# Sixteen words each of k and v, read on ScalarE's queue behind the two transfers of mu

## The chip, the cores and the metric

The kernel runs on one core of one Trainium2 chip. The metric is the device time of one execution in microseconds, as the median of the runs; one further execution is recorded by the hardware profiler, and its trace is what the prediction reads.

## What is computed

Linear attention for 8 batches of 8 heads (576 positions, 64 features per head), followed by an RWKV channel mix over the joined heads (512 features, 1024 hidden). All inputs and the output are float32. Cut to what matters:

```python
q_s = softmax(q, axis=-1)                 # over the features
k_s = softmax(k, axis=2)                  # over the positions
kv  = einsum('bhsd,bhse->bhde', k_s, v)
x   = einsum('bhsd,bhde->bhse', q_s, kv)  # then the heads side by side: [8, 576, 512]

x_prev = x shifted by one position, zeros first
xk = mu_k * x + (1 - mu_k) * x_prev
xr = mu_r * x + (1 - mu_r) * x_prev
k  = maximum(xk @ w_k, 0)
v  = k * k @ w_v
out = sigmoid(xr @ w_r) * v
```

## The kernel before

**Order.** The kernel lists some 700 steps, each with an engine, a planned cost and what it must follow. A fixed order, written out as `ORDER`, gives the steps their places; a planner (`Plan.run`) works out when each would start, and `Plan.emit` issues the instructions in order of those planned starts. Each engine runs its own instructions strictly in that order. The planned costs and latencies (`cost`, `lat`) therefore matter only where they change the order of the starts. In the gaps that the plan sees on TensorE before the first step of the channel mix, `emit` puts fill matmuls (`warm`, L320): products of the identity that nobody reads, whose number is fixed when the kernel is built.

**Tiles.** The work goes by batch `b` and half `u` (four heads). A tile of q, k or v is 128 partitions of two runs of 9 x 64 floats (576 KB), loaded by `load` (L327) on SyncE's queue; each partition's run is 2304 bytes, so that one half of a tile is a contiguous block of 128 x 2304 bytes. For batches 0 and 1 the steps are:

- ScalarE: `exp` (L332) of q and of k, out of `ldq` and `ldk` into `eq` and `ek`.
- VectorE: the sums of q (L342), their inverse, and the scaled q (`qs`, L347).
- TensorE: the transposes of `qs` (`turn_q`, L361), which ScalarE or VectorE then copy to `qT`.
- GpSimd: the cast of v to bf16 (`cast_v`, L238), out of `ldv` into `vb`, in two halves.
- TensorE: `kv` (L378), the product of `ek` and `vb`; VectorE scales it by mu into `kvm` (`weigh_kv`, L391 and L393).
- TensorE: `x_mixed` (L410), the product of `qT` and `kvm`, which gives the mixed rows at once; ScalarE or VectorE copy them to `xk` and `xr`.
- TensorE: `up` (L454) with w_k, then `gate` (L473) with w_r and `down` (L490) with w_v.

**The start.** SyncE's queue issues, in this order: q (0,0), q (0,1), k (0,0), v (0,0), k (0,1), the two halves of v (0,1), the two halves of w_k (L296), w_r (L301), and then the tiles of batch 1. ScalarE's queue begins with `load_mu` (L252): the two vectors mu_k and mu_r, each as four rows of 128 floats into the tile `mus`. The table load for exp, and then exp of q (0,0), are next on ScalarE. `mask_mu` (L263, VectorE) and `spread_mu` (L269 and L271, TensorE) make of `mus` the forms that `weigh_kv` reads; `keep_mu` (L277, L278) copies them out on ScalarE.

**Semaphores.** The build gives the transfers of both queues eight completion semaphores in turn. An instruction that issues a transfer waits until the transfer eight places before it has landed.

**The step that the change touches** is planned as

```python
a = pl.step("ACT", 0.9, load_mu, lat=4.0)
```

and `scrap`, the new tile, stands in the constants' pool between `mus` and `half`; `wk_bf`, `wr_bf` and `wv_bf` (the bf16 weights) are allocated behind them.

Of the kernel before, what the change touches and what calls it, by code (L numbers as in the profile page):

```python
# [9 lines left out]
ACT = mybir.ActivationFunctionType  # L10
# [3 lines left out]
F32 = mybir.dt.float32  # L14
# [128 lines left out]
def kernel(  # L143
# [12 lines left out]
    nc = tc.nc  # L156

    B, H, S, D = q.shape
# [3 lines left out]
    J = S // 64  # L162
# [11 lines left out]
    const = ctx.enter_context(tc.tile_pool(name="const", bufs=1))  # L174
# [19 lines left out]
    ident = const.tile([128, 128], BF16, name="ident")  # L194
    identf = const.tile([128, 128], F32, name="identf")
    mus = const.tile([8, 128], F32, name="mus")
    half = const.tile([8, 2, 64], F32, name="half")
    mine = const.tile([8, 4], F32, name="mine")
    halves = const.tile([8, 2], F32, name="halves")
# [13 lines left out]
    pl = Plan({k: len(t) for k, t in bufs.items()})  # L213
# [4 lines left out]
    def sl(kind, *key):  # L218
        if (kind, *key) not in slot:
            slot[(kind, *key)] = pl.slot(kind)  # L220
        return slot[(kind, *key)]
# [28 lines left out]
    def load_mu():  # L250
        for i, src in enumerate((moe_mu_k, moe_mu_r)):
            nc.scalar.dma_start(out=mus[4 * i:4 * i + 4, :],  # L252
                                in_=bass.AP(tensor=src.tensor, offset=src.offset,
                                            ap=[[128, 4], [1, 128]]))

    def pick():
        rows = identf[0:8, 0:8].rearrange("p (a h) -> p a h", h=2)
        nc.vector.reduce_sum(out=halves[:], in_=rows.rearrange("p a h -> p h a"), axis=AX.X)  # L258
        nc.vector.tensor_copy(out=half[:], in_=halves[:, :, None].to_broadcast((8, 2, 64)))
        nc.vector.reduce_sum(out=mine[:], in_=rows, axis=AX.X)  # L260
# [282 lines left out]


    ev["prep"] = pl.step("POOL", 1.5, prepare)
    a = pl.step("ACT", 0.9, load_mu, lat=4.0)
    p = pl.step("DVE", 0.5, pick, after=[ev["prep"]])
    p = pl.step("DVE", 0.7, mask_mu, after=[a, p], uses=[sl("th", "musb")])
    ev["mup"] = p = pl.step("PE", 2.2, spread_mu, after=[p],
# [153 lines left out]
    a = pl.step("DVE", 1.2, watch, after=[e for k, e in ev.items() if k[0] == "mix"])  # L703
    a = pl.step("PE", 0.2, gather, after=[a], uses=[sl("two", "flag")], lat=0.3)
    a = pl.step("DVE", 0.2, judge, after=[a], uses=[sl("two", "flag")])
    a = pl.step("PE", 0.1, read_flag, after=[a], lat=6.0)
# [122 lines left out]
```

## Time and profile before

| | |
|---|---|
| median of three runs | 201.28 us (201.13, 201.28, 202.19) |
| profiled execution | 200.41 us |
| its span, first to last instruction | 198.5 us |
| mean granted TensorE clock | 0.985 |
| TensorE busy | 187.5 us (94%) |
| VectorE, ScalarE, GpSimd busy | 148.1, 139.6, 31.3 us |
| moved by the DMA engines | 46.88 MB, mean 236 GB/s |

In a timeline row the columns are: start in us from the span's start, duration in us, engine, line, operation, what it writes and reads, how many instructions are merged in the row, and in brackets the idle time of the engine before it with what ended it. `SPq` and `ACTq` are the queues of SyncE and ScalarE; their rows are the issues of transfers, not the transfers. In a row of windows the columns are the stretch, its length, the busy time of PE, PEld, DVE, ACT and POOL with counts, the granted clock, the busy share of the 16 DMA engines and the GB/s that they moved. A row of a DMA queue gives packets, MB and the time of its packets as a share of 16 engines over the stretch.

### The profile page before, as it was taken

To read this page: it belongs to the slowest core of one execution; us is meant where nothing else is said; L and a number is where in the kernel's file an instruction comes from. 1 tells how busy PE (TensorE), PEld (TensorE's weight loads), DVE (VectorE), ACT (ScalarE), POOL (GpSimd) and SP (SyncE) were. 2 spreads that over 40 slices of the span, in tenths; PEclk is the share of its full clock that TensorE was granted. 3 is DMA by queue.
4 is the path that set the end of the run, shared out by engine and by line. 5 is a ranking of instruction groups with operands and counts; after the bars stand their busy time and mean duration, and the time that the engine had idled before them with its cause. 6 is when DMAs were issued, how large, how long until landed. Compare 5 with 4: busy or idle time off the path is not lost. (4 is left out here: it accounts for less than half of the span.)

```text
span 198.5 us, 4750 instructions
## 1 busy us (share of the span) xinstructions
PE 187.5 (94%) x1908; PEld 113.8 (57%) x1932; DVE 148.1 (75%) x230; ACT 139.6 (70%) x206; POOL 31.3 (16%) x43
## 2 busy tenths in 40 slices
PE   6699999999999999999999999999999999999990
PEld 4466865756546754654666546755574657564450
DVE  1978699999898999966999799799696474524230
ACT  3574699778999969968879687997857667452200
POOL 2073514622002300400016002300200000000000
PEclk9889999999999999999999999999999999999997
DMA  5999999989999499978999899984948022151555
GB/s 206 359 397 387 391 390 390 388 300 204 260 345 278 106 275 345 267 163 218 386 396 262 191 342 275 290 198 101 310 116 192 14 55 54 42 118 33 117 129 154
DMA packets 35897, 46.88 MB, mean 236 GB/s; under 512 B 16280, under 2 KB 16544, under 8 KB 35872
## 3 DMA queue, kind: packets, MB, share of 16 engines
q1 hardware_dynamic: 35456, 46.02, 78.2%
q10 hardware_dynamic: 416, 0.53, 1.0%
q8 instruction: 16, 0.26, 0.6%
q14 instruction: 9, 0.07, 0.1%
HBM read 33.56 MB, written 9.44 MB: 217 GB/s over the span
## 5 line engine op out<-in xcount | busy, mean ns | idle before, releaser
L454 PE MATMUL two<-xk,wk_bf 128*128 128x288 bf16 x512 | 68.0, 286 | 0.0
L490 PE MATMUL one<-wv_bf,k 128*128 128x512 bf16 (+1 forms) x283 | 65.1, 373 | 1.1 <-PEq L793 0.4
L454 PEld LDWEIGHTS <-wk_bf 128*128 128x128 bf16 x512 | 49.7, 98 | 17.6
L459 ACT ACTIVATE rel<-two 128x576 bf16<-128x576 f32 x64 | 40.5, 652 | 21.3 <-PE two L454 21.1
L490 PEld LDWEIGHTS <-k 128*128 128x128 bf16 x296 | 28.6, 98 | 31.0 <-issue 0.6
L238 POOL CAST vb<-ldv 128x1152 bf16<-128x1152 f32 (+1 forms) x20 | 22.3, 1131 | 101.0 <-DMA ldv<-in_v_dram 101.0
L473 PE MATMUL one<-wr_bf,xr 128*128 128x512 bf16 x133 | 35.7, 379 | 0.8 <-issue 0.3
L440 ACT ACTIVATE aw<-two,om 128x575 bf16<-128x575 f32 x48 | 32.9, 746 | 5.0 <-PE two L432 5.0
L496 DVE SCALAR_TENSOR_TENSOR ot<-th,one 128x512 f32<-128x512 f32 x33 | 22.3, 680 | 14.5 <-PE one L490 14.4
L478 ACT ACTIVATE th<-one 128x512 f32<-128x512 f32 x36 | 21.4, 600 | 12.9 <-PE one L473 12.7
L469 DVE TENSOR_TENSOR k<-rel 128x1152 bf16<-128x1152 bf16 x26 | 21.7, 839 | 5.0 <-ACT rel L459 5.0
L342 DVE TENSOR_REDUCE rs<-eq 128x18 f32<-128x1152 bf16 x16 | 21.5, 1346 | 2.1 <-ACT eq L332 2.1
L445 DVE SCALAR_TENSOR_TENSOR xk<-two,mu,aw 128x576 bf16<-128x576 f32 x24 | 19.3, 812 | 4.5 <-ACT aw L440 3.9
L347 DVE TENSOR_TENSOR qs<-eq,inv 128x1152 bf16<-128x1152 bf16 x16 | 22.3, 1396 | 0.3
L445 DVE SCALAR_TENSOR_TENSOR xr<-two,mu,aw 128x576 bf16<-128x576 f32 x24 | 19.3, 810 | 2.5 <-ACT aw L440 2.5
L332 ACT ACTIVATE eq<-ldq 128x1152 bf16<-128x1152 f32 x16 | 18.5, 1168 | 2.3 <-DMA ldq<-in_q_dram 2.3
L473 PEld LDWEIGHTS <-xr 128*128 128x128 bf16 x144 | 13.2, 98 | 11.6 <-issue 0.2
L332 ACT ACTIVATE ek<-ldk 128x1152 bf16<-128x1152 f32 x16 | 18.8, 1172 | 1.1 <-DMA ldk<-in_k_dram 1.1
L320 PE MATMUL one<-ident 128*128 128x256 bf16 x58 | 10.5, 330 | 1.8 <-DVE halves L258 1.8
L320 PEld LDWEIGHTS <-ident 128*128 128x128 bf16 x58 | 6.3, 120 | 4.1 <-DVE halves L258 1.8
L378 PEld LDWEIGHTS <-ek 64*64 64x64 bf16 x576 | 6.2, 107 | 3.2 <-ACT rel L459 1.3
L378 PE MATMUL two<-vb,ek 64*64 64x65 bf16 x576 | 7.7, 194 | 0.2 <-POOL vb L238 0.2
(54 smaller groups left out, 86.3 us busy)
## 6 DMA issues: line engine op xcount, KB each, us to landing
ldq<-in_q_dram SPq DMA_DIRECT2D x16, 576.0 KB, 6.6
ldk<-in_k_dram SPq DMA_DIRECT2D x16, 576.0 KB, 7.4
out_dram<-ot SPq DMA_DIRECT2D x66, 128.0 KB, 3.3
ldv<-in_v_dram SPq DMA_DIRECT2D x14, 576.0 KB, 9.2
k<-in_moe_w_k_dram SPq DMA_DIRECT2D x2, 1024.0 KB, 11.3
k<-in_moe_w_v_dram SPq DMA_DIRECT2D x2, 1024.0 KB, 13.7
ldv<-in_v_dram SPq DMA_DIRECT2D x4, 288.0 KB, 11.0
xr<-in_moe_w_r_dram SPq DMA_DIRECT2D x1, 1024.0 KB
```

The lines of the kernel that those rows point to most:

```text
L238: return {"DVE": nc.vector, "POOL": nc.gpsimd}[eng].tensor_copy(out=out, in_=in_)
L332: nc.scalar.activation(out=at("e" + n, b, u)[:].rearrange("p j (h d) -> p h j d", h=2), in_=at("ld" + n, b, u)[:].rearrange("p h (j d) -> ...
L342: nc.vector.reduce_sum(out=rs[:], in_=at("eq", b, u)[:].rearrange("p j (h d) -> p (j h) d", h=2), axis=AX.X)
L347: nc.vector.tensor_tensor(out=at("qs", b, u)[:].rearrange("p j (h d) -> p (j h) d", h=2), in0=at("eq", b, u)[:].rearrange("p j (h d) -> p ...
L440: nc.scalar.activation(out=at("aw", b, u, h, w)[:, 1:S], in_=x_of(b, u, h)[:, 1:S], func=ACT.Copy, scale=om[:, c:c + 1])
L445: nc.vector.scalar_tensor_tensor(out=blend(b, w)[:, 2 * u + h, :], in0=x_of(b, u, h)[:, 64:64 + S], scalar=mu[:, c:c + 1], in1=at("aw", b, ...
L454: nc.tensor.matmul(ps[:, a, 0:HS], lhsT=wk_bf[:, ct, 128 * f:128 * f + 128], rhs=xk[:, ct, HS * a:HS * a + HS], start=(ct == 0), stop=(ct ...
L459: nc.scalar.activation(out=at("rel", b, f // 2)[:, f % 2, :].rearrange("p (a c) -> p a c", a=2), in_=at("two", "up", b, f)[:, :, 0:HS], fu ...
L469: nc.vector.tensor_tensor(out=dst, in0=r[:], in1=r[:], op=ALU.mult)
L473: nc.tensor.matmul(at("one", "rp", i, m)[:], lhsT=at("xr", i)[:, ct, 128 * m:128 * m + 128], rhs=wr_bf[:, ct, :], start=(ct == 0), stop=(c ...
L490: nc.tensor.matmul(at("one", "vp", i, m, a)[:, cols], lhsT=at("k2", i)[:, f, 128 * m:128 * m + 128], rhs=wv_bf[:, f, cols], start=(f == 0) ...
L496: nc.vector.scalar_tensor_tensor(out=at(kept(i, m), i, m)[:, cols], in0=at("th", i, m)[:, cols], scalar=1.0, in1=at("one", "vp", i, m, a)[ ...
```

## The change

`load_mu` issues two more transfers behind the two of mu: from k, then from v, sixteen single words. The words stand 8 x 9 x 64 floats apart, which is every eighth partition's run of the first half of tile (0,0). They go to every eighth partition of the new tile `scrap`, k's to its first column and v's to its second. Nothing reads `scrap`. The planned cost of the step rises from 0.9 to 2.0 and its planned latency falls from 4.0 to 2.9, so that its planned end with latency stays at 4.9. The instructions of TensorE, VectorE, GpSimd and SyncE stay the same and in the same order, and ScalarE's gain the two issues. The turn of the eight semaphores moves by two from the load of q (0,1) on, and the tiles allocated behind `scrap` lie 32 bytes higher.

```diff
     mus = const.tile([8, 128], F32, name="mus")
+    scrap = const.tile([128, 2], F32, name="scrap")
     half = const.tile([8, 2, 64], F32, name="half")
...
                                 in_=bass.AP(tensor=src.tensor, offset=src.offset,
                                             ap=[[128, 4], [1, 128]]))
+        for i, src in enumerate((k, v)):
+            nc.scalar.dma_start(out=scrap[0:128:8, i:i + 1],
+                                in_=bass.AP(tensor=src.tensor, offset=src.offset,
+                                            ap=[[8 * J * D, 16], [1, 1]]))
...
-    a = pl.step("ACT", 0.9, load_mu, lat=4.0)
+    a = pl.step("ACT", 2.0, load_mu, lat=2.9)
```

## The prediction

> **What bounds the kernel now.** I read the page first, for which engine is full and when.
>
> ```profile
> span 198.5 us, 4750 instructions
> PE 187.5 (94%) x1908; PEld 113.8 (57%) x1932; DVE 148.1 (75%) x230; ACT 139.6 (70%) x206; POOL 31.3 (16%) x43
> PEclk9889999999999999999999999999999999999997
> DMA  5999999989999499978999899984948022151555
> ```
>
> TensorE is busy 94% of the span and at a high granted clock; the transfers are as full as they get in the first seventy microseconds. The change touches only the first ten, so the question is what sets the start of TensorE's unbroken work. I therefore read TensorE's timeline from 8 to 25 us next.
>
> ```profile
> 8.73 1.14 PE L361 MATMUL two<-ident,qs 128*128 128x128 bf16 x9 [1.50 <-DVE qs L347]
> 9.66 2.92 PE L320 MATMUL one<-ident 128*128 128x256 bf16 x17
> 12.76 0.48 PE L378 MATMUL two<-vb,ek 64*64 64x65 bf16 x36 [0.17 <-POOL vb L238]
> 13.17 0.68 PE L361 MATMUL two<-ident,qs 128*128 128x128 bf16 x9
> ...
> 15.33 0.39 PE L320 MATMUL one<-ident 128*128 128x256 bf16 x2
> 15.65 0.69 PE L410 MATMUL two<-qT,kvm 64*64 64x256 bf16 x20
> ...
> 19.67 5.06 PE L454 MATMUL two<-xk,wk_bf 128*128 128x288 bf16 x40
> 24.57 0.49 PE L320 MATMUL one<-ident 128*128 128x256 bf16 x3
> 24.90 0.38 PE L473 MATMUL one<-wr_bf,xr 128*128 128x512 bf16 x1
> ```
>
> This is the view that decides the case. TensorE works in a fixed order, and between the real steps it runs fill matmuls on the identity (L320), a fixed number of them. From 8.73 us on the queue is packed: the only idle entries are 1.50 us before the first transposes, which waited for q, and 0.17 us before the first k-by-v products (L378), which waited for the cast of v. Everything between is either work or fill that stays where it is when data come sooner. Next, who feeds those two waits: the timeline of the first 16 us, all engines.
>
> ```profile
> 0.84 0.58 ACTq L252 DMA_DIRECT2D mus<-in_moe_mu_k_dram  x1
> 1.46 0.26 ACTq L252 DMA_DIRECT2D mus<-in_moe_mu_r_dram  x1
> 1.76 1.28 ACT L332 ACT_TABLE_LOAD   x1 [1.76 <-issue]
> ...
> 4.43 1.16 ACT L332 ACTIVATE eq<-ldq 128x1152 bf16<-128x1152 f32 x1 [1.39 <-DMA ldq<-in_q_dram]
> 4.71 0.68 DVE L263 TENSOR_TENSOR th<-mus,mine 8x512 f32<-8x512 f32 x1 [2.63 <-DMA mus<-in_moe_mu_r_dram]
> 6.48 1.16 ACT L332 ACTIVATE eq<-ldq 128x1152 bf16<-128x1152 f32 x1 [0.89 <-DMA ldq<-in_q_dram]
> 7.31 1.36 DVE L347 TENSOR_TENSOR qs<-eq,inv 128x1152 bf16<-128x1152 bf16 x1
> 8.70 1.16 ACT L332 ACTIVATE ek<-ldk 128x1152 bf16<-128x1152 f32 x1 [1.05 <-DMA ldk<-in_k_dram]
> 10.23 3.72 POOL L238 CAST vb<-ldv 128x576 bf16<-128x576 f32 x4 [8.57 <-DMA ldv<-in_v_dram]
> ```
>
> The first q tile lands at 4.43, the second at 6.48, the first k tile at 8.70, the first v tile at 10.23: steps of 2.05, 2.22 and 1.53 us for equal sizes. So something in front of k costs up to 0.52 + 0.69 = 1.21 us against v's pace, on whichever of the 16 DMA engines is last. The windows show the same as a mean over all of them.
>
> ```profile
> 2.80:4.80 2.00, 2.00 (x12) 1.44 (x10) 0.09 (x1) 0.61 (x2) 0.00 (x0) 1.00 1.04 400
> 4.80:6.60 1.80, 1.57 (x8) 0.78 (x6) 1.57 (x2) 0.91 (x2) 0.00 (x0) 1.00 0.98 309
> 6.60:10.40 3.80, 2.30 (x18) 1.80 (x18) 3.66 (x7) 2.70 (x4) 0.17 (x1) 0.70 1.02 386
> ```
>
> The last number is GB/s, the one before it the share of the DMA engines that is busy. From 4.8 to 6.6 us, where the first k rows begin, the engines are as busy (0.98) but move 309 GB/s where 400 went before: (400 - 309) / 400 x 1.8 = 0.41 us lost per engine. After that it is 386. A first touch of k that costs time is what this looks like; v shows little of it.
>
> **The change part by part.** *The two reads, on the DMA engines.* They move 32 words and their completions. The window of the first 12 us gives the price of a packet on ScalarE's queue:
>
> ```profile
> q10 hardware_dynamic: 16, 0.00, 0.2%
> ```
>
> Sixteen packets are 0.2% of 16 engines x 12 us = 0.38 us, or 24 ns each. Some 64 more packets are 1.5 us of engine time, 0.1 us for each of the 16: at most 0.1 us later for everything behind. That is the price if a word of k costs no more than a row of mu; the bound above is a word that stalls its engine like k's first rows did, up to 1.21 us; the bound below is that they take k's stall out of the way, 0.41 us in the mean and up to 1.21 us at the last engine. No row shows such a read. I take the mean, 0.41 us sooner for k and v, because nothing but the position in the stream (k's first rows) explains the dip, and the words lie in that tile.
>
> When do they go? mu_r was issued by 1.72 and VectorE still waited for it until 4.71, about when the first q tile had landed (4.43), so a small transfer on ScalarE's queue is served behind the q rows already queued. The read of k then goes between the first and the second q tile, one tile ahead of k.
>
> *What the sooner landing is worth.* k first: its exp moves from 8.70 to about 8.3, but the ACT step behind it evicts the transposes that TensorE ends at 8.73 + 1.14 = 9.87, so ScalarE gains nothing. v: the casts move from 10.23 to about 9.8, and the product at 12.76 loses its wait for POOL. How far can it move? The fill ahead of it ends at 9.66 + 2.92 = 12.58; the L410 step at 15.65 shows that a ready step starts 0.07 before the modelled end of its fill (15.33 + 0.39 = 15.72). So it can start at 12.51: **0.25 us sooner, and no more**, whether v lands 0.41 or 1.21 us sooner. Behind it all is order and fill, so the 0.25 stays to the end.
>
> *The issues on ScalarE.* The two new issues stand ahead of the table load. At mu's 0.26 to 0.58 each they take 0.52 to 1.17 us, and the table load, from 1.76, has 1.39 us of idle time behind it before q lands: hidden, with 0.22 us left at the dear end. If the cover goes, each further 0.1 us reaches exp, the q chain and the transposes at 8.73 in full.
>
> *The waits on SyncE's queue.* The build hands out eight completion semaphores in turn and lets a transfer wait for the eighth before it. Two more transfers shift this by two from the second q load on: the second k load now waits for mu_k, the halves of v for the first q tile and mu_r, and the halves of w_k for the two small reads; from w_r on each waits for what it waited for before. SyncE's timeline of the kernel before:
>
> ```profile
> 2.90 0.59 SPq L327 DMA_DIRECT2D ldk<-in_k_dram  x1
> 3.54 0.97 SPq L327 DMA_DIRECT2D ldv<-in_v_dram  x2
> 4.55 1.64 SPq L296 DMA_DIRECT2D k<-in_moe_w_k_dram  x2
> 6.47 3.51 SPq L301 DMA_DIRECT2D xr<-in_moe_w_r_dram  x1
> ```
>
> The halves of v go out at 4.43 instead of 3.54, and w_k when the words are in, at worst with k and v, around 8.7 to 10.2 instead of 4.55. Queued behind SyncE's wait stand w_r and the next q loads. Their cover is the data already queued: GpSimd's timeline shows w_k's first use at 15.93 and its second half's at 19.18.
>
> ```profile
> 15.93 1.17 POOL L238 CAST wk_bf<-k 128x512 bf16<-128x512 f32 x2 [1.98 <-DMA k<-in_moe_w_k_dram]
> 19.18 0.62 POOL L238 CAST wk_bf<-k 128x512 bf16<-128x512 f32 x1 [2.08 <-DMA k<-in_moe_w_k_dram]
> 21.89 2.55 POOL L238 CAST wr_bf<-xr 128x1024 bf16<-128x1024 f32 x2 [2.10 <-DMA xr<-in_moe_w_r_dram]
> ```
>
> The spacing of these landings, about 3 us per half, says that the first half's rows begin to move near 13 us and the second's near 16, so an issue at 10 leaves 3 us. Taken at nothing. If that cover went, w_r is next: its casts end at 21.89 + 2.55 = 24.44 and TensorE uses them at 24.90, so 0.46 us of lateness is free there.
>
> *The tile.* `scrap` pushes the tiles allocated behind it 32 bytes up, the three weight tiles among them. No row tells whether a matmul minds; I take nothing, and leave it in the tail.
>
> **The sum.** The profiled execution took 200.41 us, its span of 198.5 plus 1.91. Minus 0.25, plus 0 for issues, waits and tile: 200.16. The median of the runs, 201.28, stands 0.87 above that execution, so the forecast is 201.28 - 0.25 = 201.03, said as **201.0 us**. A difference of 0.5% (1.0 us) is about what a measurement here can tell from no change; the three runs lie 1.06 us apart.
>
> **Rivals.** *The stall only moves* (chance 0.25). The words meet the stall instead of k's rows, one tile sooner, and the engine that waits for them carries nothing else meanwhile. Then the second q tile lands later, by 0.41 us (6.48 to 6.9), k and v when they did, plus the 0.1 of the packets. The second q tile can afford it: its exp ends at 7.64 and ScalarE then idles until 8.70. v has no cover, so the 0.1 counts: 201.4 us. For it: the busy share stayed at 0.98 while the rate fell, so a stalled engine counts as busy and does nothing else. Against it: a pending word need not hold a row of another queue. [...]
>
> *Slower: the words pay and save nothing* (0.20). If the dip belongs to the rows read and not to a first touch of the tensor, the words stall in their own right and k's rows again. The place is the first cast of v on POOL at 10.23, which TensorE already waits for; from the first 0.1 us on, lateness there counts in full. The price is a k-like stall at the last engine, 1.21 us: 202.5 us; at the mean, 0.41, it is 201.7. [...] Against it: the steps between later tiles are back at 1.53.
>
> *Slower: the issues outgrow their cover* (0.06). At 0.82 each, w_k's price on SyncE (1.64 for two), the table load ends 0.25 us late: 201.5; it would need 1.2 each to pass 1 us. [...]
>
> *Faster by over 1 us* (0.09). The granted clock is part of it: transposes take 1.14 us at 8.73 and 0.68 at 13.17, so TensorE ran slow around 9 us. If sooner data kept the clock up, those transposes give 0.46 us, the fills more, and v's 1.21 us would then count in full: 200.1. Against it: the idle 1.50 us before 8.73 hangs on q, which the change leaves alone.
>
> **How the numbers follow.** The forecast has 0.40, the rivals 0.25, 0.20, 0.06 and 0.09. The range runs from 200.2, near the fast rival, to 202.5, the slow one's price. Within 0.5% means 200.27 to 202.29: the forecast and the moved stall (0.65) less 0.12 for the scatter of the runs, plus the cheap ends of the slow rivals (0.07) make 0.60. Slower by over 0.5%: 0.19 from the slow rivals and 0.05 from scatter, 0.24. Faster: 0.09 and 0.07, 0.16.
>
> **What would show it.** Right: the rate from 4.8 to 6.6 us is up towards 400, k's exp starts before 8.5 and v's cast before 10.0, L378 starts at about 12.5 with no wait for POOL, and the first L454 at about 19.4. Moved stall: the dip sits before 4.8 us and v's cast is at 10.2 to 10.3. Slow: v's cast after 10.6 and L378 behind it. The issues: the table load ends after 4.43. Wrong altogether: L454 first starts where it did, and the time differs by over 1 us, which the tile's place or the later waits would have to explain.

## The result, and the profile after

The changed kernel takes 202.84 us (median of 15 runs, 201.74 to 204.22), the kernel before, run beside it, 201.61 us (15 runs). The ratio is **1.0085, 95% interval 1.0058 to 1.0112**: slower by about 1.7 us, or by 1.2 us if the two medians are taken (their quotient is 1.0061), where 201.0 us, no measurable change, was forecast. 202.84 lies above the top of the stated range, 202.5. The ratio leaves out executions that lie more than 1.5% above the fastest of the same kernel. The profiled execution took 202.59 us, its span 200.8.

First the same parts of the page, now of the changed kernel.

```profile
span 200.8 us, 4752 instructions
PE 188.6 (94%) x1908; PEld 113.9 (57%) x1932; DVE 148.9 (74%) x230; ACT 139.6 (70%) x206; POOL 33.9 (17%) x43
PEclk9969999999999999999999999999999999999996
DMA  6999999989998399997997999955948031242535
```

TensorE is busy 1.1 us longer than before, of which 0.9 us lie ahead of the channel mix, in time in which it was idle before; GpSimd is busy 2.6 us longer, the rest and the clock (0.983, before 0.985) are about as they were. So the 2.3 us by which the span grew have to be looked for in waits. The prediction looked at the start. TensorE's timeline there, changed kernel (its lines lie 5 further on than before):

```profile
8.82 0.68 PE L366 MATMUL two<-ident,qs 128*128 128x128 bf16 x9 [1.13 <-DVE qs L352]
9.34 3.46 PE L325 MATMUL one<-ident 128*128 128x256 bf16 x17
12.81 0.60 PE L383 MATMUL two<-vb,ek 64*64 64x65 bf16 x36
...
19.78 5.06 PE L459 MATMUL two<-xk,wk_bf 128*128 128x288 bf16 x40
```

The channel mix (L459) starts at 19.78 us instead of 19.67: 0.11 us of the loss, no more. What feeds it, from the timeline of all engines and the windows:

```profile
1.76 0.58 ACTq L257 DMA_DIRECT2D scrap<-in_k_dram  x1
2.38 0.60 ACTq L257 DMA_DIRECT2D scrap<-in_v_dram  x1
3.01 1.28 ACT L337 ACT_TABLE_LOAD   x1 [3.01 <-issue]
4.53 1.16 ACT L337 ACTIVATE eq<-ldq 128x1152 bf16<-128x1152 f32 x1 [0.24 <-DMA ldq<-in_q_dram]
6.33 1.16 ACT L337 ACTIVATE eq<-ldq 128x1152 bf16<-128x1152 f32 x1 [0.64 <-DMA ldq<-in_q_dram]
8.76 1.16 ACT L337 ACTIVATE ek<-ldk 128x1152 bf16<-128x1152 f32 x1 [1.27 <-DMA ldk<-in_k_dram]
10.27 3.74 POOL L239 CAST vb<-ldv 128x576 bf16<-128x576 f32 x4 [8.61 <-DMA ldv<-in_v_dram]
```

```profile
2.80:4.80 2.00, 2.00 (x12) 1.41 (x10) 0.00 (x0) 1.55 (x2) 0.00 (x0) 1.00 1.03 400
4.80:6.60 1.80, 1.80 (x6) 0.91 (x5) 1.56 (x2) 1.17 (x2) 0.00 (x0) 1.00 0.99 292
```

k and v land at 8.76 and 10.27 us, 0.06 and 0.04 later than before, and the dip between 4.8 and 6.6 us is still there, at 292 GB/s (309 before). The words brought nothing.

Now the other end of the span, of which the prediction shows no row. `last` holds the blocks of the output that come last. VectorE, ScalarE's queue and SyncE's queue, first before, then after:

```profile
188.05 0.60 ACT L478 ACTIVATE th<-one 128x512 f32<-128x512 f32 x1 [0.34 <-PE one L473]
189.94 0.69 DVE L496 SCALAR_TENSOR_TENSOR last<-th,one 128x512 f32<-128x512 f32 x1 [3.00 <-PEq L793]
190.89 0.60 SPq L506 DMA_DIRECT2D out_dram<-ot  x1
192.26 3.40 ACTq L506 DMA_DIRECT2D out_dram<-last  x5
193.62 1.77 SPq L506 DMA_DIRECT2D out_dram<-last  x3
193.69 0.42 DVE L496 SCALAR_TENSOR_TENSOR last<-th,one 128x256 f32<-128x256 f32 x1 [0.52 <-PE one L490]
```

```profile
189.35 0.60 ACT L483 ACTIVATE th<-one 128x512 f32<-128x512 f32 x1 [0.34 <-PE one L478]
190.37 2.04 SPq L511 DMA_DIRECT2D out_dram<-ot  x2
191.24 0.69 DVE L501 SCALAR_TENSOR_TENSOR last<-th,one 128x512 f32<-128x512 f32 x1 [3.00 <-PEq L798]
194.71 3.18 ACTq L511 DMA_DIRECT2D out_dram<-last  x5
194.99 0.42 DVE L501 SCALAR_TENSOR_TENSOR last<-th,one 128x256 f32<-128x256 f32 x1 [0.52 <-PE one L495]
195.02 1.86 SPq L511 DMA_DIRECT2D out_dram<-last  x3
```

The first `last` block is computed at 189.94 + 0.69 = 190.63 us before and 191.24 + 0.69 = 191.93 after. ScalarE's queue stores it 1.63 us later before (192.26), but 2.78 us later after (194.71). The five stores then follow each other, and the span ends 2.9 us behind the end of the last one's issue in both. From VectorE's last finish to the start of the very last instruction, 0.05 us ahead of the end of the span, pass 4.36 us before and 5.33 after; this stretch is called the end from here on. So 0.97 us of the loss in these two traces lies behind VectorE's last finish, 190 us after the edit.

Another 1.1 us of the two spans' difference of 2.3 is one wait of TensorE at about 110 us. It is no part of the change: the first experiment below, which has no reads and is as fast as before, shows the same row, and the kernel with the largest loss (two late words) does not. Of the kernels of the table below, four of the seven without the loss have it in their trace, and two of the five with it. Changed kernel, the tile alone, two late words:

```profile
L459 PE MATMUL two<-xk,wk_bf 128*128 128x288 bf16 x512 | 68.0, 286 | 1.1 <-ACT rel L464 1.1
```

```profile
L455 PE MATMUL two<-xk,wk_bf 128*128 128x288 bf16 x512 | 68.0, 286 | 1.1 <-ACT rel L460 1.1
```

```profile
L460 PE MATMUL two<-xk,wk_bf 128*128 128x288 bf16 x512 | 68.0, 286 | 0.0
```

**What happens at the end.** Near the end all engines take a branch on a flag (L793 before, L798 after), GpSimd first, at 176.3 us before, SyncE last, at 191.54. One arm, `general`, would compute everything again for inputs out of range; it holds 114 transfers on SyncE's queue and is not run. The other arm must leave the eight completion semaphores as the first would, so in it SyncE waits for each of the eight, always from the first to the eighth, and raises it. Behind the branch come eight stores of `last`, five on ScalarE's queue, three on SyncE's, and each uses one of the eight in turn. A store of ScalarE can therefore not be issued before SyncE has passed its semaphore: ScalarE's first goes out 0.07 us behind SyncE's raise of the second semaphore before (192.19, 192.26) and 0.08 us behind its raise of the fourth after (194.63, 194.71). And SyncE passes none that stands behind the semaphore of a store that has not landed: the last completion of SyncE's last store before the branch is recorded at 193.41 us before, and SyncE passes its semaphore, the seventh, at 193.42; after, the two are 194.33 and 194.35, and the semaphore is the first. The turn moves by one with every transfer on these two queues: one more transfer brings that store from the seventh semaphore to the eighth (experiment 7), two bring it to the first, four to the third (experiment 11). The waits of SyncE behind the branch, before and after (us in total, times, longest):

```profile
SPq L793 <- SPq L793: 1.5, 3, 0.8
```

```profile
SPq L798 <- SPq L798: 1.8, 1, 1.8
```

Before, the waits are three, the first of them the 0.53 us from the start of the branch to the first instruction behind it, and ScalarE's first stores go out between them; after, there is one, ahead of everything.

### The profile page after: what moved, and what is told of

Same layout as the page of the kernel before. It is cut to its first block, busy times and chain, and to the rows that moved or that the text cites. A ratio compares the mean times of both kernels' runs of the same rounds, so it can differ in the third digit from the quotient of the medians.

```text
span 200.8 us, 4752 instructions
## 1 busy us (share of the span) xinstructions
PE 188.6 (94%) x1908; PEld 113.9 (57%) x1932; DVE 148.9 (74%) x230; ACT 139.6 (70%) x206; POOL 33.9 (17%) x43
## 5 line engine op out<-in xcount | busy, mean ns | idle before, releaser
L459 PE MATMUL two<-xk,wk_bf 128*128 128x288 bf16 x512 | 68.0, 286 | 1.1 <-ACT rel L464 1.1
L459 PEld LDWEIGHTS <-wk_bf 128*128 128x128 bf16 x512 | 49.8, 98 | 18.6 <-issue 1.0
L239 POOL CAST vb<-ldv 128x1152 bf16<-128x1152 f32 (+1 forms) x20 | 24.5, 1245 | 100.0 <-DMA ldv<-in_v_dram 78.5
L352 DVE TENSOR_TENSOR qs<-eq,inv 128x1152 bf16<-128x1152 bf16 x16 | 23.3, 1459 | 0.3
L325 PE MATMUL one<-ident 128*128 128x256 bf16 x58 | 11.4, 351 | 1.8 <-DVE halves L263 1.8
L383 PEld LDWEIGHTS <-ek 64*64 64x64 bf16 x576 | 6.3, 109 | 3.2 <-ACT rel L464 1.3
L383 PE MATMUL two<-vb,ek 64*64 64x65 bf16 x576 | 7.8, 196 | 0.0
```

The lines of the kernel that those rows point to most:

```text
L239: return {"DVE": nc.vector, "POOL": nc.gpsimd}[eng].tensor_copy(out=out, in_=in_)
L352: nc.vector.tensor_tensor(out=at("qs", b, u)[:].rearrange("p j (h d) -> p (j h) d", h=2), in0=at("eq", b, u)[:].rearrange("p j (h d) -> p ...
L459: nc.tensor.matmul(ps[:, a, 0:HS], lhsT=wk_bf[:, ct, 128 * f:128 * f + 128], rhs=xk[:, ct, HS * a:HS * a + HS], start=(ct == 0), stop=(ct ...
```

## The experiments

Three theories stood at the outset: the tile moves the weights; the words of k and v cost; the turn of the semaphores moves. The kernels were run in four groups (1 to 4, 5 to 8, 9 to 12, 13 and 14), each beside the kernel before on one chip. Behind each ratio stands its 95% interval.

**1. The tile alone.** `scrap` and the planned costs, without the reads.

```diff
-        for i, src in enumerate((k, v)):
-            nc.scalar.dma_start(out=scrap[0:128:8, i:i + 1],
...
```

> The tile and the planned costs of the change, without the two reads. Theory A (the 32-byte shift of the tiles behind the new one costs the loss): about 1.7 us slower than before, with matmul durations or casts that differ from before's. Theories B (the waits on the eight semaphores in turn) and C (the reads themselves): equal to before within 0.3%.

Measured: 0.9999 (0.9974 to 1.0025), 4.35 us from VectorE's last finish to the end. The tile costs nothing measurable.

**2. The reads, with the tile allocated last**, so that no other tile moves.

```diff
-    scrap = const.tile([128, 2], F32, name="scrap")
     half = const.tile([8, 2, 64], F32, name="half")
...
+    scrap = const.tile([128, 2], F32, name="scrap")
```

> The two reads of k and v as in the change, into a tile allocated behind all others, so that no other tile moves. Theory A: equal to before. Theories B and C: about 1.7 us slower than before, like the change.

Measured: 1.0047 (1.0021 to 1.0073), 5.56 us at the end. The loss comes with the reads. It is smaller than the 1.7 us expected, but the interval overlaps that of the change.

**3. The words out of mu** instead of k and v: the transfers stay, what they read does not.

```diff
-        for i, src in enumerate((k, v)):
+        for i, src in enumerate((moe_mu_k, moe_mu_r)):
...
-                                            ap=[[8 * J * D, 16], [1, 1]]))
+                                            ap=[[32, 16], [1, 1]]))
```

> The change, but the sixteen words of each transfer come from mu_k and mu_r (32 floats apart) and not from k and v: same issues on ScalarE, same turn of the semaphores, same tile, no touch of k or v. Theory B (turn of the semaphores) and theory A: about 1.7 us slower than before. Theory C (words of k and v): equal to before within 0.3%, and the dip of the rate at 5 us is where it was before.

Measured: 1.0066 (1.0039 to 1.0094), 5.89 us at the end. It does not matter what the words are.

**4. The words of k and v on GpSimd's queue**, whose transfers are not in the turn of the eight.

```diff
-            nc.scalar.dma_start(out=scrap[0:128:8, i:i + 1],
+            nc.gpsimd.dma_start(out=scrap[0:128:8, i:i + 1],
```

> The same words of k and v, issued on GpSimd's queue, which is idle between 1.7 and 10.2 us: ScalarE issues two transfers fewer, and the eight semaphores of the other two queues turn as in the kernel before. Theory B: equal to before, or faster by up to 0.25 us. Theory C: about 1.7 us slower. If the two issues on ScalarE alone cost it (exp of q from 4.43 to 4.53), at most 0.1 us of the loss goes.

Measured: 0.9991 (0.9965 to 1.0016), 3.80 us at the end. The same reads outside the turn cost nothing measurable, and save nothing measurable either.

The next four put the theory of the order of waits against one by which early reads on ScalarE's queue cost as such.

**5. Two late words, no early reads.** In the tile-alone kernel SyncE's queue reads two words where it idles.

```diff
     def dma_turn_q(b, u):
+        if (b, u) == (NM, 0):
+            for n in range(2):
+                nc.sync.dma_start(out=scrap[1 + n:2 + n, 0:1],
+                                  in_=bass.AP(tensor=k.tensor, offset=k.offset + 128 * n,
+                                              ap=[[1, 1], [1, 1]]))
```

> The early reads are left out (the tile stays); instead SyncE's queue reads two single words of k at about 34 us, in an idle stretch of 8.8 us before its first transposing transfer. Theory of the order of waits: what costs is where the last store before the branch stands in the turn of eight semaphores. Behind its branch SyncE waits for the eight one after the other, always from the first to the eighth, and raises each; ScalarE's stores of `last` each need one of them. The last store before the branch sits on the seventh in the kernel before, and two transfers more, wherever they stand, bring it to the first: ScalarE's first store of `last` comes over 1 us later, 5.3 to 5.9 us pass between VectorE's last finish and the end (4.36 before), ratio 1.0045 to 1.0085. Theory of the early reads (the two transfers cost by where they stand, behind mu on ScalarE's queue): ratio 0.998 to 1.002, 3.8 to 4.4 us at the end.

Measured: 1.009 (1.0054 to 1.0125), 5.27 us at the end, one wait of 1.8 us. Two transfers in an idle stretch at 34 us cost as much as the change does. The start has no part in it.

**6. A whole turn, words on SyncE.** The changed kernel with the same loop for six words.

```diff
+            for n in range(6):
+                nc.sync.dma_start(out=scrap[1 + n:2 + n, 0:1],
...
```

> The changed kernel, with six single words of k read on SyncE's queue at about 34 us besides: eight transfers more than before, so that the turn of eight comes out whole. Theory of the order of waits: the last store before the branch is back on the seventh semaphore; 3.8 to 4.4 us from VectorE's last finish to the end, ratio to the kernel before 0.998 to 1.0025, although everything the change added is still there. Theory of the early reads: the loss stays, ratio 1.0045 to 1.0085, and 5.3 to 5.9 us at the end.

Measured: 1.0056 (1.0028 to 1.0083), 5.60 us at the end. **A miss**: the last store was back on the seventh semaphore and the loss stayed. SyncE's wait behind the branch is one piece here too, although the issue of the first semaphore's store had ended 7.4 us before that wait passed:

```profile
SPq L803 <- SPq L803: 2.0, 1, 2.0
```

Either the early reads cost after all, or the six instructions more on SyncE did this. Experiments 9, 10, 13 and 14 take it up.

**7. One read.** k's words alone.

```diff
-        for i, src in enumerate((k, v)):
+        for i, src in enumerate((k,)):
```

> The changed kernel with the words of k alone, one transfer more than before. Theory of the order of waits: the last store before the branch comes to stand on the eighth semaphore, behind all that ScalarE's five stores of `last` need; no loss, ratio 0.997 to 1.002, 3.8 to 4.4 us at the end, ScalarE's first store of `last` no later behind SyncE's branch than the 0.72 us of before. Theory of the early reads: half of the two, ratio 1.002 to 1.004.

Measured: 1.0004 (0.9977 to 1.003), 4.02 us at the end. One transfer costs not half of two but nothing: the last store then stands on the eighth semaphore. A price per read would have given 1.002 to 1.004, whose lower half the interval touches; the end shows nothing of it.

**8. The stores first.** The changed kernel; in `ORDER` the stores of (2, 4) and (3, 1), steps 635 and 665, go ahead of those that still wait for VectorE.

```diff
-675 663 508 509D 678 664 679 680 665 635 683 ...
+635 675 663 508 509D 678 664 665 679 680 683 ...
```

> The changed kernel with both its reads; of the stores that SyncE issues before its branch, the pair of (2, 4), ready at about 171.6 us, moves ahead of that of (3, 3), into SyncE's idle time, and the pair of (3, 1), ready at 183.5 us, ahead of that of (3, 4), for which SyncE waits until 185.2 us. In the kernel before, these two pairs stand behind it and take four issues of 0.64 us. Theory of the order of waits: SyncE then issues its last store at about 187.5 us on the scale of the kernel before instead of 190.9, it lands before the first half of `last` is computed (190.6 us), and the turn no longer matters: ScalarE's stores wait for VectorE alone; 3.4 to 3.6 us from VectorE's last finish to the end, ratio to the kernel before 0.994 to 0.998. Theory of the early reads: their loss at the start stays, less what the new order of stores brings against the changed kernel: ratio 1.000 to 1.004.

Measured: **0.9948 (0.9916 to 0.998)**, 3.46 us at the end: faster than before, with both reads and the bad turn in it. The end of its timeline:

```profile
191.90 0.69 DVE L501 SCALAR_TENSOR_TENSOR last<-th,one 128x512 f32<-128x512 f32 x1 [3.00 <-PEq L798]
192.62 4.00 ACTq L511 DMA_DIRECT2D out_dram<-last  x5
195.66 0.42 DVE L501 SCALAR_TENSOR_TENSOR last<-th,one 128x256 f32<-128x256 f32 x1 [0.52 <-PE one L495]
```

ScalarE's first store goes out at 192.62, when its block is ready (191.90 + 0.69 = 192.59); it no longer waits for SyncE to pass a semaphore.

**9. A whole turn, words on ScalarE.** As 6, with the six words issued on ScalarE ahead of relu steps 29, 41, 49 and 60.

```diff
+    WORDS, nth = {29: 1, 41: 1, 49: 2, 60: 2}, [0]
     def relu(b, f):
+        nth[0] += 1
+        for n in range(WORDS.get(nth[0], 0)):
+            r = 1 + n + nth[0] % 4 * 2
+            nc.scalar.dma_start(out=scrap[r:r + 1, 0:1],
...
```

> The changed kernel with six single words of k besides, now on ScalarE's queue in stretches where it waits for TensorE (at about 87, 122, 146 and 172 us); eight transfers more than before, and SyncE has as many instructions ahead of its branch as in the changed kernel. With the six on SyncE's queue the loss had stayed, although its last store before the branch was on the seventh semaphore: SyncE passed even the first wait only 2.01 us behind its branch. Theory of the order of waits, with a second effect of SyncE's six instructions more in that kernel: here six waits pass from 0.53 us behind the branch, the stall is at the seventh, 3.8 to 4.4 us from VectorE's last finish to the end, ratio 0.998 to 1.0025. Theory of the early reads: ratio 1.0045 to 1.0085, 5.3 to 5.9 us at the end.

Measured: 1.0026 (0.9996 to 1.0055), 4.27 us at the end, the first wait passing after 0.53 us. The ratio is 0.0001 above what was expected, and the upper part of its interval lies outside, but the end is as before, with all that the change added still there. SyncE's waits are again in three pieces:

```profile
SPq L806 <- SPq L806: 1.4, 3, 0.7
```

**10. Eight words on SyncE, no early reads** (the loop of 5 with eight).

```diff
-            for n in range(2):
+            for n in range(8):
```

> No early reads (the tile stays); eight single words of k on SyncE's queue at about 34 us: the turn comes out whole, and SyncE has eight instructions more ahead of its branch. If these instructions are the second effect, the first wait behind the branch passes about 2 us after it, as with six, and 5.0 to 5.9 us pass from VectorE's last finish to the end, ratio 1.003 to 1.0085. If the order of waits is all there is, 3.8 to 4.4 us and 0.998 to 1.0025. Theory of the early reads: 0.998 to 1.002 too, there being none.

Measured: 1.0032 (1.0005 to 1.0058), 4.20 us at the end; the first wait passed after 0.97 us. The end fits the order of waits alone, the ratio fits a second effect, and the first wait lies between, so alone it settles nothing. The 0.3% by which it is slower is not seen at its end and stays open.

**11. Four late words on ScalarE, no early reads** (the loop of 9 with two words each ahead of relu 49 and 60). The last store comes to the third semaphore.

```diff
-    WORDS, nth = {29: 1, 41: 1, 49: 2, 60: 2}, [0]
+    WORDS, nth = {49: 2, 60: 2}, [0]
```

> No early reads (the tile stays); four single words of k on ScalarE's queue, at about 146 and 172 us, so that the last store before the branch stands on the third semaphore of the eight; SyncE has as many instructions as in the kernel before. Theory of the order of waits: two waits pass from 0.53 us behind the branch, the third is held until that store has landed, about 1.9 us behind its issue's end, and ScalarE's first store of `last`, on the sixth, comes behind it: 5.2 to 5.9 us from VectorE's last finish to the end, ratio 1.0035 to 1.0085. Theory of the early reads: 0.998 to 1.002, 3.8 to 4.4 us.

Measured: 1.0071 (1.0046 to 1.0097), 5.19 us at the end. The third wait was the last that was held, as expected; it passed 1.95 us behind the end of the last store's issue, and ScalarE's first store came behind it. The first wait passed after 1.07 us, not 0.53. Three waits are held, as before, but all of them ahead of ScalarE's stores, the first of which goes out 2.76 us behind its finished block:

```profile
194.66 3.22 ACTq L515 DMA_DIRECT2D out_dram<-last  x5
```

```profile
SPq L802 <- SPq L802: 1.8, 3, 1.0
```

**12. The stores first, no reads.** The edit of 8 in the tile-alone kernel.

```diff
-675 663 508 509D 678 664 679 680 665 635 683 ...
+635 675 663 508 509D 678 664 665 679 680 683 ...
```

> The kernel before (with the tile) with only the new order of SyncE's stores, no reads: the last store before the branch stands on the seventh semaphore, as before. Theory of the order of waits: ScalarE's stores of `last` wait for VectorE alone, as in the kernel with the reads and this order; 3.4 to 3.6 us from VectorE's last finish to the end, ratio to the kernel before 0.993 to 0.998, and the reads make no difference. Theory of the early reads: 0.0045 to 0.0085 less than the 0.9948 of the kernel with the reads, 0.986 to 0.990.

Measured: **0.9941 (0.9914 to 0.9968)**, 3.22 us at the end, less than the 3.4 to 3.6 expected. With the end cleared, the kernel with reads (0.9948) and that without are the same within their intervals.

**13 and 14. Six and two, four and four.** A whole turn without early reads: six words on SyncE and two on ScalarE, and four on each.

```diff
-            for n in range(8):
+            for n in range(6):
...
+    WORDS, nth = {49: 2}, [0]
```

```diff
-            for n in range(8):
+            for n in range(4):
...
+    WORDS, nth = {49: 2, 60: 2}, [0]
```

> No early reads (the tile stays); six single words of k on SyncE's queue at about 34 us and two on ScalarE's at about 146 us: a whole turn, the last store before the branch on the seventh semaphore. If six instructions more on SyncE ahead of its branch made the loss of the kernel with the reads and six words there, it is here too: the first wait behind the branch passes about 2.0 us after it, 5.2 to 5.9 us from VectorE's last finish to the end, ratio 1.0035 to 1.0085. If that loss came from the early reads together with the words, the first wait passes after 0.53 us, 3.8 to 4.4 us at the end, ratio 0.998 to 1.0025.

> As the kernel with six and two, but four words on SyncE's queue and four on ScalarE's: the same turn, with two instructions less on SyncE. If it depends on where the branch falls in SyncE's instructions, four are below the point at which it begins (two more had left no mark of it, six and eight did): first wait after 0.53 us, 3.8 to 4.4 us at the end, ratio 0.998 to 1.0025. If every instruction more costs, the first wait passes after 1 to 1.5 us, ratio 1.002 to 1.005.

Measured: six and two 1.0057 (1.0021 to 1.0093), 5.36 us at the end; four and four 1.0014 (0.9982 to 1.0045), 4.14 us. The six bring the miss of experiment 6 again without an early read, the four do not. SyncE's waits, six, then four:

```profile
SPq L807 <- SPq L807: 2.0, 1, 2.0
```

```profile
SPq L807 <- SPq L807: 1.5, 3, 0.8
```

So a second effect exists: with six instructions more on SyncE ahead of its branch it is there, with four it is not, and with eight (experiment 10) the first wait is late by less (0.97 us). The changed kernel has none more, and its first wait passes 1.94 us behind the last store's issue, as the wait for the last store does before.

**All together**, from the semaphore and issue events of the traces. "First wait": us from SyncE's branch to the first of the eight waits passing. "First store": us from SyncE's branch to ScalarE's first store of `last`. "End": as above.

| kernel | last store's semaphore | more on SyncE | first wait | first store | end | ratio |
|---|---|---|---|---|---|---|
| before | 7th | 0 | 0.53 | 0.72 | 4.36 | 1 |
| 1 tile alone | 7th | 0 | 0.53 | 0.72 | 4.35 | 0.9999 |
| 4 words on GpSimd | 7th | 0 | 0.53 | 0.72 | 3.80 | 0.9991 |
| 7 one read | 8th | 0 | 0.53 | 0.80 | 4.02 | 1.0004 |
| 9 whole turn, ScalarE | 7th | 0 | 0.53 | 0.72 | 4.27 | 1.0026 |
| 14 four and four | 7th | 4 | 0.52 | 0.71 | 4.14 | 1.0014 |
| 10 eight on SyncE | 7th | 8 | 0.97 | 1.17 | 4.20 | 1.0032 |
| **after** | 1st | 0 | 1.88 | 2.24 | 5.33 | 1.0085 |
| 2 tile last | 1st | 0 | 1.83 | 2.19 | 5.56 | 1.0047 |
| 3 words of mu | 1st | 0 | 1.92 | 2.28 | 5.89 | 1.0066 |
| 5 two late words | 1st | 2 | 1.89 | 2.25 | 5.27 | 1.0090 |
| 11 four late words | 3rd | 0 | 1.07 | 2.22 | 5.19 | 1.0071 |
| 6 whole turn, SyncE | 7th | 6 | 2.01 | 2.22 | 5.60 | 1.0056 |
| 13 six and two | 7th | 6 | 2.06 | 2.26 | 5.36 | 1.0057 |
| 8 stores first, reads | 1st | 1 | 1.81 | 2.54 | 3.46 | 0.9948 |
| 12 stores first | 7th | 1 | 0.52 | 2.54 | 3.22 | 0.9941 |

The seven kernels of the first block have a mean end of 4.16 us, the five in which the turn blocks (after, 2, 3, 5, 11) one of 5.45: 1.29 us more, which is 0.64% of 201.6. The mean of those five ratios is 1.0072, that of the first block's 1.0009: a difference of 0.63%. In the mean over these kernels the end accounts for the loss. For the changed kernel alone its one trace shows 0.97 us there and 0.11 us at the start, of the 1.2 to 1.7 us that the runs show; the rest is not settled.

## Why the prediction was wrong, step by step

**The step that failed** is "The waits on SyncE's queue". It saw that two more transfers move the turn of the eight semaphores by two, followed this from q (0,1) to w_r, said that "from w_r on each waits for what it waited for before", and took it at nothing. In the middle of the kernel that holds. At the end it does not: there the semaphores are waited for in their own order, not in that of the transfers, and the price is 1.29 us. Experiments 3, 5 and 11 make that loss without a word of k or v at the start; 4 and 7 keep words and are without it; 9, which restores the turn, cannot be told from no change. What the prediction lacked was any row of the last ten microseconds: the timeline of SyncE's and ScalarE's queues there shows, before the change, ScalarE's first store going out 1.63 us behind a finished block, which asks for a reason. Its last sentence did name the later waits as one of two causes if all else failed.

**The gain at the start** was mis-sized too: 0.25 us were forecast, and the channel mix came 0.11 us later. "Because nothing but the position in the stream explains the dip, and the words lie in that tile" does not hold: with the words in, the rate from 4.8 to 6.6 us is 292 GB/s instead of about 400, k lands at 8.76 us, not 8.3, and v at 10.27, not 9.8. The early reads with the turn left alone (experiment 4) and with the end cleared (8 against 12) bring nothing measurable. What makes the dip is still open; a first touch that sixteen words take away it is not. L383 did lose its wait for GpSimd, but only because the fill ahead of it took 3.46 us instead of 2.92. The prediction took the length of that fill as fixed. The granted clock had moved: it was 0.93 instead of 0.52 from 8 to 10 us, where the transposes took 0.68 us instead of 1.14, and 0.50 instead of 0.62 from 10 to 12 us, under the fill. The fill now ends at 9.34 + 3.46 = 12.80 and L383 starts at 12.81, so v could not have moved it by landing sooner.

**Right by their sizes.** The issues on ScalarE: 0.58 and 0.60 us, the table load over at 3.01 + 1.28 = 4.29 with 0.24 us of idle left (0.22 was worked out for the dear end). The start of the semaphores: the halves of v went out at 4.52 us (4.43 said). w_k followed at 6.50 us, sooner than the 8.7 to 10.2 of the worst case, and its cover held, nearly: its casts came at 16.01 and 19.35 us, 0.08 and 0.17 later. The tile: 0.9999. The price of the words, at most 0.1 us: in the first 12 us ScalarE's queue carried 80 packets instead of 16, as forecast, and they took 0.4% of the engines' time instead of 0.2%, which is about 0.02 us for each engine.

**The rivals.** None had the mechanism. "The words pay and save nothing" has a time near what came (202.5), for a reason that fell: its sign that would show it, v's cast after 10.6, did not appear. "The issues outgrow their cover" and "faster by clock" did not happen; "the stall only moves" is nearest for the start alone.

## What to carry to other kernels

A transfer that is added did not cost only where it stood: two words at 34 us made this kernel 0.9% slower, with 5.27 us at the end instead of 4.36 (experiment 5). Where the build hands out completion semaphores in turn, it moves the semaphore of every later transfer, and the bill comes at a place that waits for them in a fixed order, here a branch, where it was 1.29 us in the mean. So look there in the trace, and test with a transfer that does nothing, in an idle stretch. The better cure is not to tune the number of transfers but to have the last stores before such a place issued early: two pairs of stores that were ready, moved ahead of pairs that had to wait for VectorE, made the kernel 0.6% faster than before (0.9941, 0.9914 to 0.9968) and took the turn's effect away.

## What the runs showed of the hardware

The wait for SyncE's last store (128 KB, out of 64 partitions) passed 1.80 to 2.23 us behind the end of that store's issue in the kernels whose waits show it (1.94 us before, 1.94 after, 1.95 in experiment 11): a store issued last was never a short wait.

From the start of SyncE's branch to the first instruction behind it passed 0.52 to 0.53 us where that had nothing to wait for. With six instructions more ahead of it, it took 2.01 and 2.06 us (experiments 6 and 13), with four 0.52, with eight 0.97; why 0.97 is not known. In the two with six, a packet of instructions (8 KB, on the queue that the page lists as "q14 instruction") started 0.43 and 0.47 us behind the branch; with four it started 1.31 us behind it, long after the first wait had passed (before, with none more, 1.26), and with eight one started 0.85 us ahead of it. The late first waits thus came with a packet that started just behind the branch. No run moved that packet by itself, so what held SyncE there is not shown.
